# Which PSUM bank a small matrix product gets: in turn, or whichever has been free longest

## The chip, the cores and the metric

The kernel runs on one core of a Trainium2 chip, in float32 (the matmul operands are split into a rounded high part and a low remainder). The metric is the device time of one execution in microseconds (us). Three runs of the kernel before took 1197.13, 1197.44 and 1198.53 us; the median, 1197.44, is the time that the prediction is made for.

## The reference, cut to what matters

Four layers are applied to `x`, 2048 positions by 576 channels: A, B, A, B, each with its own layer norm and a residual.

```python
def A(x):   # Fourier mixing: only the real part is kept
    a, b = x @ dft_hid_re.T, x @ dft_hid_im.T
    return dft_seq_re @ a - dft_seq_im @ b
def B(x):   # gate by a long convolution; k, v, filters do not depend on x
    kv = shift_conv(k, 4 taps) * v
    y = irfft(rfft(kv, 4096) * rfft(ssm_k, 4096))[:2048] + kv * ssm_D
    return x * y
x = x + A(layernorm(x)); x = x + B(layernorm(x))
x = x + A(layernorm(x)); x = x + B(layernorm(x))
```

The convolution result `y` is the same in both B layers, so it is made once.

## The kernel before, in words

TensorE does all transforms as matmuls (line 75, the helper `mm`). PSUM has eight banks of 128 x 512 float32 here: four accumulators `s0` to `s3` and one for the remaining channels, `rm`, serve the large sequence transform (128x512 products, tiles `s` and `rm` in the profile). The last three banks, `bk`, serve every **small product**:

- `f1_products` (line 436): the first transform stage of the convolution. Two banks at once, six matmuls on half the rows of the array, evacuated by ScalarE (line 448). 52 pairs in the first 200 us.
- the middle of the convolution, for 64 blocks of the spectrum: `mid_kernel` (a product `pk`, evacuated by ScalarE through `act`, line 509, then three more ScalarE copies), `mid_signal` (a product `px`, read by three VectorE multiplications with the filter from `mid_kernel`, lines 528 to 530) and, two blocks later, `mid_inverse` (a product `pv`, evacuated by ScalarE, line 509, and stored to DRAM). Three matmuls of 288 columns each.
- `i2_products`: the last stage of the convolution, six matmuls, evacuated by ScalarE (line 509).
- `hidden`: the channel transform of a finished block of rows, 27 matmuls of 288 columns, added to the residual by VectorE (line 284). Two halves per block of 128 rows, in both A layers.
- the remainder accumulators `rem` of the second A layer (`strassen`), which hold a bank for several steps.

Before the change `bank()` (line 79) hands out three tiles, made once for the whole kernel, in turn: the product with number p in the program takes bank p mod 3, whatever the others do. It can start when the product p-3 has been read out.

The order of the work has two parts. The program's text interleaves the streams by hand: the loop over the large transform's steps n (16 per half block) calls the small work from generators (`br` for the convolution, `pending` for `hidden`), with counts such as `MID_FROM = 47` and `I2_FIRST = 37`. From this text the language's planner fixes, ahead of the run, the order of instructions on each engine: by its own reckoning of times it takes, of the instructions whose operands and banks are ready, the one that stands earliest in the text. So a large matmul of a later step goes ahead of a small product that still waits, and products may start in another order than they stand. At run time every engine works its list strictly in that order, with semaphores for what it needs. `behind(...)` adds an order on one engine: all `act` instructions of the middle run on ScalarE in the order of the text.

At the end of a half block (n = 47, 79, 111) the large transform cannot go on until the `hidden` halves of the block before have read the tile `u` that it will overwrite; the loop calls all that are left there.

Of the kernel before, what the change touches and what calls it, by code (L numbers as in the profile page):

```python
# [10 lines left out]
F32 = mybir.dt.float32  # L11
# [4 lines left out]
P = 128  # L16
# [5 lines left out]
NT = 512  # L22
# [43 lines left out]
def fnet_h3_kernel(ctx: ExitStack, tc: tile.TileContext, x, c_mat, w_re, w_im, k_pad, v, shift_k,  # L66
# [4 lines left out]
    psp = ctx.enter_context(tc.tile_pool(name="psp", bufs=1, space=bass.MemoryType.PSUM))  # L71
    dr = ctx.enter_context(tc.tile_pool(name="dr", bufs=1, space=bass.MemoryType.DRAM))

    def mm(ps, lhsT, rhs, first, last, more=False):
        return nc.tensor.matmul(ps, lhsT, rhs, start=first, stop=last, skip_group_check=more).ins  # L75

    banks, given = [psp.tile([P, NT], F32, tag=f"b{i}", name=f"bk{i}") for i in range(3)], [0]

    def bank():
        given[0] += 1  # L80
        return banks[(given[0] - 1) % 3]

    acc4 = [psp.tile([P, NT], F32, tag=f"s{i}", name=f"s{i}") for i in range(4)]
    last_pair = [acc4[2:]]
# [13 lines left out]
    @contextmanager  # L98
    def behind(*instructions):
        with ExitStack() as stack:  # L100
            for i in instructions:
                stack.enter_context(tc.issue_after(i))
            yield
# [36 lines left out]
    def two(v):  # L140
        return v.rearrange("p (a n) -> p a n", a=2)
# [131 lines left out]
    def hidden(us, tb, jj, xres, done, late=False):  # L273
        j = TB * tb + jj
        r = ring["res"]()
        (load_after if late else nc.sync.dma_start)(r, xres(j))
        for hf in range(2):
            ps = bank()
            cs = slice(hf * HD, (hf + 1) * HD)
            for ch in range(9):  # L280
                for n, (a, b) in enumerate(((0, 0), (0, 1), (1, 0))):
                    mm(ps[:, :HD], us[ch][:, a, jj * P:(jj + 1) * P], W[ch][:, b, cs],
                       ch == 0 and n == 0, ch == 8 and n == 2)
            added[:] = [nc.vector.tensor_tensor(r[:, cs], r[:, cs], ps[:, :HD], OP.add).ins]  # L284
            yield
        done(j, r)
# [59 lines left out]
    def branch():  # L346
# [89 lines left out]
            return tuple(paired)  # L436

        def f1_products(j, fc, xf, at, n, so, to):
            ps = [bank()[:, :n] for _ in range(2)]
            last = seq[-1:]  # L440
            for k, (a, b) in enumerate(((0, 1), (0, 0), (1, 0))):
                for i in (1, 0):
                    half = slice(i * HP, (i + 1) * HP)
                    with behind(*last):
                        last = [mm(ps[i], fc[half, a, :], xf[b][half, at:at + n], k == 0, k == 2)]
            so = two(ring[so]())
            for i in range(2):
                stored[:] = [nc.scalar.activation(so[:, i, :], ps[i], AF.Copy).ins]  # L448
            nc.scalar.dma_start(t_d[:, j::J, to:to + n], so)

        conv, made_ops, visits = convolve(), 0, []
        def visit(half):
            if visits and visits[0][0] <= half:
                f1_products(*visits.pop(0)[1:])
# [42 lines left out]
        def mid_half(df, o):  # L497
            ps = bank()
            mm(ps[:, :HD], mc[:, 0, :], df[0][:, o:o + HD], True, False)
            mm(ps[:, :HD], mc[:, 0, :], df[1][:, o:o + HD], False, False)  # L500
            mm(ps[:, :HD], mc[:, 1, :], df[0][:, o:o + HD], False, True)
            return ps
# [653 lines left out]
```

## Time and profile before

| what | before |
|---|---|
| median of three runs | 1197.44 us |
| the profiled execution's own time | 1199.58 us |
| its span, first to last instruction | 1197.8 us |
| TensorE (PE) busy | 1175.3 us, 6248 matmuls |
| VectorE (DVE) / ScalarE (ACT) busy | 839.2 / 660.5 us |
| granted TensorE clock, mean | 0.998 |
| small products `bk`: PE busy | 464.4 us |

The profile is of one execution. Each row of the timeline merges neighbouring instructions of a kind: start, time, engine, line, tiles written <- read, count, and in brackets the engine's idle time before it and what ended it. Matmuls overlap in the array, so a row's time is longer than what it adds; the pace is read from one row's start to the next. PEld is the weight load that goes before each matmul. A wait of PEld that fits under the matmul still running costs nothing.

### The profile page before, as it was taken

To read this page: it belongs to the slowest core of one execution; us is meant where nothing else is said; L and a number is where in the kernel's file an instruction comes from. 1 tells how busy PE (TensorE), PEld (TensorE's weight loads), DVE (VectorE), ACT (ScalarE), POOL (GpSimd) and SP (SyncE) were. 2 spreads that over 40 slices of the span, in tenths; PEclk is the share of its full clock that TensorE was granted. 3 is DMA by queue.
4 is the path that set the end of the run, shared out by engine and by line. 5 is a ranking of instruction groups with operands and counts; after the bars stand their busy time and mean duration, and the time that the engine had idled before them with its cause. 6 is when DMAs were issued, how large, how long until landed. Compare 5 with 4: busy or idle time off the path is not lost.

```text
span 1197.8 us, 18057 instructions
## 1 busy us (share of the span) xinstructions
PE 1175.3 (98%) x6248; PEld 996.6 (83%) x6248; DVE 839.2 (70%) x1498; ACT 660.5 (55%) x1311; POOL 75.1 (6%) x116
## 2 busy tenths in 40 slices
PE   7999999999999999999999999999999999999997
PEld 5776667888888888888988898888888888789997
DVE  7899983679777677675347766865776777774764
ACT  7865555669877668775435666634444445450210
POOL 2210000000000000001101121000000000001111
PEclk9999999999999999999999999999999999999999
DMA  9869898446656667648957676872772787795621
GB/s 337 294 196 315 260 300 268 158 133 182 221 189 199 212 174 209 199 138 270 289 200 237 222 256 216 272 259 71 224 277 71 218 278 257 242 317 173 218 88 41
DMA packets 142845, 259.84 MB, mean 217 GB/s; under 512 B 15649, under 2 KB 43553, under 8 KB 142754
## 3 DMA queue, kind: packets, MB, share of 16 engines
q1 hardware_dynamic: 102674, 205.45, 52.9%
q10 hardware_dynamic: 33168, 42.63, 10.2%
q0 software_dynamic: 6912, 10.62, 3.5%
q8 instruction: 49, 0.80, 0.3%
q14 instruction: 42, 0.34, 0.1%
HBM read 191.99 MB, written 66.65 MB: 216 GB/s over the span
## 4 chain that ended last, share of the span: by engine, by line
PE 76%; ACT 2%; DVE 2%; DMA 1%; issue 1%; POOLq 0%; DVEq 0%; ACTq 0%
PE s L75 42%; PE bk L75 30%; PE rm L75 4%; ACT flts L509 1%; DMA flts<-in_c_mat 0%; ACT u L95 0%; ACT mid L509 0%; DVE u L96 0%; DVE mid L515 0%; DVE flts L529 0%; ACT mats L95 0%; DVE flts L530 0%; DMA xa<-flts 0%; DMA mid<-td 0%; DVE flts L528 0%
## 5 line engine op out<-in xcount | busy, mean ns | idle before, releaser
L75 PE MATMUL s<-mats 128*128 128x512 f32 x2088 | 541.2, 395 | 1.5 <-ACT mats L192 0.9
L75 PEld LDWEIGHTS s<-mats 128*128 128x128 f32 x2088 | 381.4, 188 | 84.1 <-issue 10.9
L96 DVE TENSOR_TENSOR mats<-flts,mats 128x512 fp32r<-128x512 f32 x206 | 140.7, 687 | 64.3 <-ACT mats L95 63.8
L95 ACT ACTIVATE mats<-flts 128x512 fp32r<-128x512 f32 x206 | 128.5, 628 | 85.4 <-PE bk L75 28.4
L75 PE MATMUL bk<-mid 128*128 128x288 f32 x768 | 135.5, 301 | 3.0 <-ACT flts L509 1.6
L75 PEld LDWEIGHTS bk<-mid 128*128 128x128 f32 x768 | 116.9, 188 | 24.1 <-ACT flts L509 7.0
L75 PE MATMUL bk<-w,u 128*128 128x288 f32 x864 | 120.6, 295 | 0.9 <-ACT w L237 0.5
L75 PEld LDWEIGHTS bk<-w,u 128*128 128x128 f32 x864 | 117.8, 188 | 3.5 <-ACT w L237 0.8
L515 DVE TENSOR_TENSOR mid<-flts,mid 128x576 fp32r<-128x576 f32 (+1 forms) x149 | 93.4, 628 | 34.3 <-ACT mid L509 30.5
L509 ACT ACTIVATE flts<-bk 128x288 f32<-128x288 f32 x160 | 62.2, 404 | 88.8 <-PE bk L75 82.4
L75 PE MATMUL rm<-mats 128*128 128x512 f32 x304 | 95.1, 391 | 0.0
L509 ACT ACTIVATE flts<-flts 64x288 f32<-64x288 f32 x192 | 85.0, 443 | 5.5
L509 ACT ACTIVATE mid<-flts 128x576 fp32r<-128x576 f32 (+1 forms) x148 | 80.4, 575 | 7.2 <-DMA flts<-td 3.1
L284 DVE TENSOR_TENSOR flts<-flts,bk 128x288 f32<-128x288 f32 x48 | 21.7, 453 | 69.9 <-PE bk L75 69.9
L448 ACT ACTIVATE flts<-bk 128x384 f32<-128x384 f32 (+1 forms) x104 | 43.1, 462 | 45.7 <-PE bk L75 45.6
L75 PE MATMUL bk<-mats 128*128 128x288 f32 (+1 forms) x376 | 67.8, 317 | 0.0
L75 PEld LDWEIGHTS rm<-mats 128*128 128x128 f32 x304 | 57.1, 188 | 12.1 <-issue 0.2
L75 PE MATMUL s<-t,mats 128*128 128x512 f32 x264 | 65.0, 390 | 0.0
L181 POOL TENSOR_TENSOR flts<-flts 128x1 f32<-128x1 f32 x35 | 28.7, 820 | 523.1 <-DVE flts L180 523.0
L75 PE MATMUL bk<-mats,t 128*128 128x288 f32 (+1 forms) x368 | 59.3, 303 | 0.0
L75 PEld LDWEIGHTS bk<-mats 128*128 128x128 f32 x376 | 55.6, 188 | 3.4
L75 PEld LDWEIGHTS s<-t,mats 128*128 128x128 f32 x264 | 49.4, 188 | 10.6 <-DVE t L96 0.4
(145 smaller groups left out, 1465.3 us busy)
## 6 DMA issues: line engine op xcount, KB each, us to landing
flts<-in_c_mat SPq DMA_DIRECT2D x148, 256.0 KB, 3.5
ph<-in_c_mat SPq DMA_DIRECT2D x54, 512.0 KB, 4.7
flts<-in_c_mat SPq DMA_DIRECT2D x30, 512.0 KB, 5.0
flts<-td SPq DMA_DIRECT2D x53, 288.0 KB, 3.1
td<-flts ACTq DMA_DIRECT2D x36, 384.0 KB, 4.6
vd<-flts ACTq DMA_DIRECT2D x64, 144.0 KB, 2.4
flts<-vd SPq DMA_DIRECT2D x32, 288.0 KB, 4.6
mid<-in_i2c POOLq DMA_DIRECT2D x32, 256.0 KB, 4.9
```

The costliest lines, as they stand in the source:

```text
L75: return nc.tensor.matmul(ps, lhsT, rhs, start=first, stop=last, skip_group_check=more).ins
L95: a = nc.scalar.activation(h, src, AF.Copy).ins
L96: return a, nc.vector.tensor_tensor(l, src, h.bitcast(F32), OP.subtract).ins
L181: pows.append(nc.gpsimd.tensor_tensor(rs, ve, mhalf, OP.pow).ins)
L284: added[:] = [nc.vector.tensor_tensor(r[:, cs], r[:, cs], ps[:, :HD], OP.add).ins]
L448: stored[:] = [nc.scalar.activation(so[:, i, :], ps[i], AF.Copy).ins]
L509: last_act.append(nc.scalar.activation(*args, **kw).ins)
L515: nc.vector.tensor_tensor(l, src, h.bitcast(F32), OP.subtract)
```

## The change

The three fixed tiles stay, renamed `bf`, and `turn()` gives them out to `f1_products` alone. Every other small product asks a pool for a tile with the tag `b`, three at most at a time. The planner then chooses: a product gets a bank when it is its turn to start and a bank of the three has been read out, and the one that has been free longest. No instruction is added or taken away. The eight banks are used up by either scheme, so the pool's tiles can be placed only where the fixed ones have been released, after the first stage's last product.

```diff
-    banks, given = [psp.tile([P, NT], F32, tag=f"b{i}", name=f"bk{i}") for i in range(3)], [0]
-
-    def bank():
+    banks, given = [psp.tile([P, NT], F32, tag=f"b{i}", name=f"bf{i}") for i in range(3)], [0]
+
+    def turn():
         given[0] += 1
         return banks[(given[0] - 1) % 3]
+
+    def bank():
+        return psp.tile([P, NT], F32, tag="b", bufs=3, name="bk")
...
         def f1_products(j, fc, xf, at, n, so, to):
-            ps = [bank()[:, :n] for _ in range(2)]
+            ps = [turn()[:, :n] for _ in range(2)]
```

## The prediction, made before the run

> **What bounds the kernel now.** I read the page first: the span, the busy times and the chain of work that ended last.
>
> ```profile
> span 1197.8 us, 18057 instructions
> PE 1175.3 (98%) x6248; PEld 996.6 (83%) x6248; DVE 839.2 (70%) x1498; ACT 660.5 (55%) x1311; POOL 75.1 (6%) x116
> PE 76%; ACT 2%; DVE 2%; DMA 1%; issue 1%; POOLq 0%; DVEq 0%; ACTq 0%
> ```
>
> TensorE is busy for 98% of the span and the chain runs through it: PE is the bound, and the number of matmuls (6248) does not change. So the change is worth only the time in which PE stands still for a bank. Where that is, the busy time by stage tells (the first three rows: start:end, length, PE, PEld, DVE, ACT, POOL, clock, DMA; the last is the same for instructions on `bk` alone).
>
> ```profile
> 215.00:262.00 47.00, 44.91 (x301) 40.67 (x299) 32.57 (x67) 30.84 (x68) 0.00 (x0) 1.00 0.44 145
> 262.00:330.00 68.00, 67.59 (x351) 57.83 (x351) 57.29 (x114) 59.67 (x130) 0.00 (x0) 1.00 0.61 192
> 612.00:800.00 188.00, 188.00 (x932) 161.05 (x931) 125.74 (x282) 105.71 (x206) 18.80 (x32) 1.00 0.72 239
> ...
> 215.00:262.00 47.00, 40.57 (x274) 36.94 (x272) 15.40 (x35) 6.96 (x17) 1.00 0.44 145
> ```
>
> From 612 to 800 us PE has no gap at all. Between 215 and 262 us 274 of its 301 matmuls write a shared bank, and there it idles most. The first stage keeps its fixed banks, and it ends before the others begin:
>
> ```profile
> L75 PE MATMUL bk<-f1r x312: 286/333/606, 6.6 to 198.1; 64*128 64x384 f32 x108, 64*128 64x288 f32 x48
> L448 ACT ACTIVATE flts<-bk x104: 388/487/501, 9.4 to 198.8; 128x384 f32<-128x384 f32 x72, 128x288 f32<-128x288 f32 x32
> L509 ACT ACTIVATE flts<-bk x160: 387/410/423, 218.2 to 612.3; 128x288 f32<-128x288 f32 x160
> L528 DVE TENSOR_TENSOR flts<-bk,flts x64: 445/456/458, 220.0 to 546.0; 128x288 f32<-128x288 f32 x64
> L529 DVE TENSOR_TENSOR flts<-bk,flts x64: 458/459/462, 220.5 to 546.9; 64x288 f32<-64x288 f32 x64
> L530 DVE TENSOR_TENSOR flts<-bk,flts x64: 450/451/454, 220.9 to 547.4; 64x288 f32<-64x288 f32 x64
> L284 DVE TENSOR_TENSOR flts<-flts,bk x48: 442/453/456, 216.4 to 1161.5; 128x288 f32<-128x288 f32 x48
> ```
>
> The last four kinds are what frees a bank later on: 0.41 us on ScalarE for `pk`, `pv` and the last stage, 0.456 + 0.459 + 0.451 = 1.37 us on VectorE for `px`, 0.45 us for `hidden`. Who waits for them between 199.8 and 620 us, matmuls and weight loads:
>
> ```profile
> PE bk L75 <- ACT flts L509: 1.6, 5, 0.5
> PE bk L75 <- DVE flts L284: 0.8, 1, 0.8
> PE bk L75 <- DVE flts L530: 0.3, 1, 0.3
> ...
> PEld bk L75 <- ACT flts L509: 7.0, 18, 0.8
> PEld bk L75 <- DVE flts L530: 4.4, 14, 0.7
> PEld bk L75 <- DVE flts L284: 1.5, 2, 1.2
> PEld bk L75 <- DVE mid L515: 1.1, 5, 0.2
> ```
>
> 34 weight loads wait for a read-out (18 + 14 + 2, 12.9 us). That is a ceiling: part of it passes under matmuls still running. What is really lost I take from the pace.
>
> ```profile
> 207.07 2.88 PE L75 MATMUL s<-mats 128*128 128x512 f32 x12
> 209.79 0.62 PE L75 MATMUL rm<-mats 128*128 128x512 f32 x2
> ...
> 240.46 3.77 PE L75 MATMUL bk<-w,u 128*128 128x288 f32 x27
> 244.06 0.29 PE L75 MATMUL bk<-mid 128*128 128x288 f32 x1
> ```
>
> A large matmul takes (209.79 - 207.07) / 12 = 0.227 us, a small one (244.06 - 240.46) / 27 = 0.133 us. Now one wait of the kind that the change is about:
>
> ```profile
> 333.40 1.07 PE L75 MATMUL s<-mats 128*128 128x512 f32 x4
> 334.78 0.66 PE L75 MATMUL bk<-mid 128*128 128x288 f32 x3 [0.31 <-DVE flts L530]
> 335.28 1.09 PE L75 MATMUL s<-mats 128*128 128x512 f32 x4
> ...
> 333.11 0.69 ACT L509 ACTIVATE flts<-bk 128x288 f32<-128x288 f32 x2
> ...
> 333.31 0.46 DVE L528 TENSOR_TENSOR flts<-bk,flts 128x288 f32<-128x288 f32 x1
> 334.28 0.45 DVE L530 TENSOR_TENSOR flts<-bk,flts 64x288 f32<-64x288 f32 x1
> ```
>
> The four large matmuls let PE go at 333.40 + 4 x 0.227 = 334.31; the small one starts at 334.78, when line 530 has ended (334.73): **0.47 us lost**. The three then take 0.50 instead of 0.40 us: 0.10 more, since weights are not loaded ahead during a stall. And ScalarE had emptied the two other banks by 333.80, almost 1 us earlier. The product stood before the wrong door.
>
> In the stage of the `hidden` halves it looks otherwise:
>
> ```profile
> 244.19 0.40 PE L75 MATMUL rm<-mats 128*128 128x512 f32 x1
> 244.86 1.06 PE L75 MATMUL bk<-mid 128*128 128x288 f32 x6 [0.27 <-ACT flts L509]
> 246.15 0.53 PE L75 MATMUL bk<-mid 128*128 128x288 f32 x2 [0.24 <-ACT flts L509]
> ...
> 244.40 0.41 ACT L509 ACTIVATE flts<-bk 128x288 f32<-128x288 f32 x1 [1.26 <-PE bk L75]
> ...
> 244.26 0.46 DVE L284 TENSOR_TENSOR flts<-flts,bk 128x288 f32<-128x288 f32 x1 [1.22 <-PE bk L75]
> 245.57 0.45 DVE L530 TENSOR_TENSOR flts<-bk,flts 64x288 f32<-64x288 f32 x1
> ```
>
> PE is free at 244.19 + 0.227 = 244.42 and waits 0.44 us, but the earliest read-out ends at 244.72 (line 284), the next at 244.81 (line 509), the third at 246.02 (line 530): all three banks are held. Choice alone wins 0.1 us here.
>
> Worked so, 17 of the 34 waits delay PE by 0.1 us or more, the first and the last of them these:
>
> ```profile
> 216.92 0.40 PE L75 MATMUL bk<-mid 128*128 128x288 f32 x1 [0.77 <-DVE flts L284]
> ...
> 429.63 0.67 PE L75 MATMUL bk<-mid 128*128 128x288 f32 x3
> ```
>
> Together 5.66 us, and 17 restarts of 0.104 us, 1.77 us: **7.4 us is all that banks cost after the first stage**. By kind: (a) 6 waits with another bank already empty, 1.42 us and 0.62 us of restarts, 2.05 us; (b) 4 waits of the `hidden` stage between 244 and 253 us with all banks held, 1.89 and 0.42, 2.3 us; (c) 7 others with all banks held, 2.34 and 0.73, 3.1 us.
>
> **The change part by part.** *First stage.* Same tiles in the same turn: 0 us. *Handing over.* The pool's first product can start once a fixed bank is released, at about 198.8 + 0.49 = 199.3 us; the first `hidden` product starts at 210.25. 11 us of cover: 0. *Instructions, DMAs, queues.* None is added; SP's and POOL's lists hold the same DMAs, and the stores on ScalarE's queue follow the same read-outs: 0 by themselves. *The turn goes.* The six waits of (a) end: -2.05 us. Those of (c) stay, as no bank is free: 0.
>
> *The planner's order.* This is the part that the trace of before does not show. A product no longer has to follow number p-3, so the planner may start them in another order, and the list of every engine can shift. In (b) a `hidden` half stands earlier in the text than the `pk` and `px` that overtook it because its fixed bank was held; with any bank it goes at the first release, and its 27 matmuls (3.6 us) give ScalarE and VectorE time to empty the others. The bounds: -2.3 us (all of (b)) and, the other way, the price of the slower rival below, +12.3 us. Rows nearest to it are the four waits themselves, so I take half of them, -1.15 us.
>
> *What is late next.* A product that gets its bank earlier may find its operands late. The nearest row is the wait for line 515, the low part of an operand: 5 times, 1.1 us, 0.22 us each. For the ten products of (a) and (b) that is 0 to 2.2 us; as such a wait mostly passes under the matmul before, I take 0.5 us.
>
> *Behind a waiting product* stands everything on PE, in its fixed order; nothing on the other engines is queued behind it except the read-outs of that product.
>
> One rule of the Trainium skill speaks against (a). The page Perfetto Trace Analysis, section Optimization Strategy, says that a gap which keeps recurring can mean that there is not enough PSUM for the next tile, and points to the number of buffers. The number stays three here, so by that rule the gain would be 0 and the time 1197.4 us. For (b) and (c) the trace agrees: all three were held. For (a) it does not: two of three were empty at 333.80.
>
> **The sum** against the profiled execution: 1199.58 - 2.05 - 1.15 + 0.5 = 1196.9 us. That execution stands 2.14 us above the median of the runs, 1197.44; for a run I therefore forecast **1194.7 us**, 0.23% less.
>
> **The rivals.**
> *All bank waits go* (the new order also clears (b) and (c)): 1197.44 - 7.4 = 1190.0 us. For it: from 215 to 262 us the `hidden` halves are ready filling work. Against it: in 11 of 17 waits no bank was empty, and three banks remain three.
>
> *Nothing changes*: the read-outs finish mostly in turn, so the bank free longest is the one whose turn it is; or the six waits become waits for operands. 1197.4 us. For it: 11 of the 17 waits, and 17 of 34 that cost nothing today. Against it: the six rows like 334.78. The Trainium skill's page Perfetto Trace Analysis, section Matmuls, asks that independent groups rotate through the banks, which the fixed turn already does; by that alone there is nothing to win.
>
> *Slower: `px` takes the banks ahead of `pv`.* With fixed banks, between 262 and 550 us, `px`, `pk` and `pv` each keep to one bank. From a pool the `pk` and `px` of the next block take banks as soon as their operands are split, and a `pv` that becomes ready next finds none until a `px` has gone through lines 528 to 530: 1.37 us. ScalarE must read that `pv` before the next `pk`, so the chain of the middle is stretched too. It counts only where PE has no large matmul to fill with, above all from 215 to 262 us: 274 matmuls there, less 7 halves of 27 and a few that are left of the first, are about 81, or 27 products of three, 9 blocks. 9 x 1.37 = 12.3 us if each is exposed; with half of that 1197.4 + 6 = 1203.4 us, at most 1209.7. It decides from the point where a `pv` wait outlasts the matmuls that are ready behind it in the list. For it: VectorE and ScalarE work 57 and 60 of 68 us from 262 to 330, so read-outs do queue. Against it: `pv` stands earlier in the text, so it wins whenever it is ready at the release.
>
> **How the numbers follow.** A measurement of this kernel can tell about 0.2%, 2.4 us, from no change. Forecast case 0.45 (1192.5 to 1196.8; 0.27 of it faster by over 0.2%, 0.18 within); all waits gone 0.10, faster; nothing changes 0.12 (0.02, 0.08, 0.02); slower 0.33 (0.02 within, 0.31 slower). Faster 0.39, same 0.28, slower 0.33. The range goes from just under the best case, 1189.5, to 1205.5, past the middle of the slower case; what it leaves out is the tail up to 1209.7.
>
> **What would show it.** Right: PE's waits for line 530 in 330 to 440 us gone, the gaps between 244 and 253 us shorter, the first stage unchanged up to 198 us, and PE still without a gap from 612 to 800 us. Wrong: new gaps of PE with `pv` products behind line 530, PE's waits for line 515 growing past 2 us, large matmuls (`s`, `rm`) waiting for line 95 or 515 because the lists of ScalarE and VectorE shifted, or gaps after 612 us, where I assume none.

## The result and the profile after

Over nine runs of each on the same chip the changed kernel took 1195.03 us (1193.42 to 1195.99) and the kernel before 1198.53 us (1197.13 to 1199.86). The ratio is 0.9970, with a 95% interval from 0.9960 to 0.9981: 3.6 us less, at least 2.3 and at most 4.8. A second comparison, seven runs against 25, gave 0.9968 (0.9957 to 0.9979). Forecast were 1194.7 us and a gain of 2.7 us.

The page of the changed kernel: its profiled execution took 1195.03 us.

```profile
span 1193.3 us, 18055 instructions
PE 1172.4 (98%) x6248; PEld 996.3 (83%) x6248; DVE 840.3 (70%) x1498; ACT 661.1 (55%) x1311; POOL 75.6 (6%) x116
PE 76%; ACT 3%; DVE 1%; issue 1%; DMA 0%; POOLq 0%; ACTq 0%; DVEq 0%; SPq 0%
```

PE is still busy for 98% and still carries 76% of the chain. A change of 0.3% can't be seen on the page; the table by stage shows it (same columns as before the change):

```profile
215.00:262.00 47.00, 46.01 (x309) 42.42 (x308) 35.84 (x73) 32.51 (x71) 0.00 (x0) 1.00 0.48 153
262.00:330.00 68.00, 67.61 (x350) 57.58 (x349) 56.49 (x111) 59.48 (x128) 0.00 (x0) 1.00 0.58 183
612.00:800.00 188.00, 188.00 (x928) 160.85 (x927) 128.10 (x285) 107.49 (x209) 18.80 (x32) 1.00 0.73 244
800.00:1050.00 250.00, 250.00 (x1103) 206.54 (x1102) 176.56 (x234) 113.64 (x187) 0.00 (x0) 1.00 0.63 209
```

In the stage of the `hidden` halves PE now does 309 matmuls where it did 301, with 46.01 us busy instead of 44.91. From 262 to 330 us (67.61 us busy, 67.59 before) and from 612 to 800 us (188.00 in both) PE's busy time has not moved. One row is a surprise. From 800 to 1050 us PE has no idle time left, and in the kernel before it had 1.09 us there:

```profile
800.00:1050.00 250.00, 248.91 (x1098) 205.70 (x1097) 174.52 (x232) 113.74 (x188) 0.00 (x0) 1.00 0.63 206
```

Who the weight loads wait for between 199.8 and 620 us (us in total, times, longest):

```profile
PEld bk L75 <- ACT flts L512: 7.6, 19, 0.8
...
PEld bk L75 <- DVE mid L518: 1.0, 4, 0.3
...
PEld bk L75 <- DVE flts L533: 0.5, 2, 0.3
```

All lines of the changed kernel stand three further down, so L533 is the old line 530 and L512 the old 509. The waits behind line 530 fell from 14 (4.4 us) to two (0.5 us). Those behind the read-outs of ScalarE did not fall: 18 with 7.0 us became 19 with 7.6 us. Both rows are the case in small: a product no longer stands before the slowest door, but it often stands before another.

**Where the time went** is counted best at points where both kernels have issued exactly the same set of matmuls: the start of the next one, changed kernel less kernel before. I did this for three pairs of profiles, the first and two repetitions of both kernels.

| stretch (time in the kernel before) | first pair | second | third |
|---|---|---|---|
| 217 to 258 us (260 in the first pair): `hidden` stage | -2.00 us | -2.00 | -1.96 |
| 258 to 590 us | -0.53 | -0.08 | -0.61 |
| 590 to 1040 us | +0.23 | +0.87 | +0.57 |
| 1040 to 1050 us | -1.28 | -1.26 | -1.02 |

Before that the pairs differ by -0.7 to +2.7 us, both ways, through loads at the start and a wait for the splitting of weights at 213 us (lines 237 and 238), which is longer in one execution than in the next. In the second pair the changed kernel lost 0.4 us between 462 and 471 us, which hides its gain in the second row. What the third row loses is lost at one place: at 749 us in the second and third pair (0.86 and 0.57 us), at 863 us in the first (0.2 us). The lists of all engines are the same there in both kernels, and no run shows why.

### The profile page after: what moved, and what is told of

Same layout as the page of the kernel before. It is cut to its first block, busy times and chain, and to the rows that moved or that the text cites. A ratio compares the mean times of both kernels' runs of the same rounds, so it can differ in the third digit from the quotient of the medians.

```text
span 1193.3 us, 18055 instructions
## 1 busy us (share of the span) xinstructions
PE 1172.4 (98%) x6248; PEld 996.3 (83%) x6248; DVE 840.3 (70%) x1498; ACT 661.1 (55%) x1311; POOL 75.6 (6%) x116
## 4 chain that ended last, share of the span: by engine, by line
PE 76%; ACT 3%; DVE 1%; issue 1%; DMA 0%; POOLq 0%; ACTq 0%; DVEq 0%; SPq 0%
PE s L75 43%; PE bk L75 30%; PE rm L75 4%; ACT flts L512 1%; ACT mid L512 1%; ACT u L98 0%; DMA wd<-w 0%; ACT mats L98 0%; DVE mid L518 0%; DVE flts L534 0%; DVE flts L533 0%; DVE flts L531 0%; DVE flts L532 0%; DVE mats L99 0%; POOLq L1155 0%
## 5 line engine op out<-in xcount | busy, mean ns | idle before, releaser
L75 PE MATMUL bk<-mid 128*128 128x288 f32 x768 | 131.9, 298 | 2.4 <-ACT flts L512 1.6
L512 ACT ACTIVATE flts<-bk 128x288 f32<-128x288 f32 x160 | 62.1, 404 | 86.8 <-PE bk L75 77.7
L512 ACT ACTIVATE flts<-flts 64x288 f32<-64x288 f32 x192 | 85.0, 443 | 5.5
L512 ACT ACTIVATE mid<-flts 128x576 fp32r<-128x576 f32 (+1 forms) x148 | 80.4, 575 | 7.6 <-DMA flts<-td 3.2
L451 ACT ACTIVATE flts<-bf 128x384 f32<-128x384 f32 (+1 forms) x104 | 43.2, 463 | 45.6 <-PE bf L75 45.5
```

Of the source, the lines that this page charges most:

```text
L512: last_act.append(nc.scalar.activation(*args, **kw).ins)
```

## The experiments

Twelve experiments ran, four of them repeats of the two kernels, in four groups, each group on one chip with its own runs of the kernel before (medians 1198.36 to 1198.95 us; the group of the last profile has a single one).

**Both kernels once more.** No edit.

> The kernel before, profiled once more. In its first profile TensorE lost 0.68 + 0.66 us at 213.7 and 214.5 us to the weight splits (lines 237 and 238) and 1.25 us at 1045.8 us to line 96 of the second A layer; in the changed kernel's profile these are 0.18 + 0.66 us and 0. Theory 'chance of one execution': the wait at 1045 us is under 0.3 us or at another place this time, and the first one moves by some tenths. Rival 'the banks of the remainder accumulators cause it': it stands again at the same place with 1.0 to 1.5 us. The 17 bank waits (5.7 us together) repeat within 0.3 us under both.

> The changed kernel once more, for its time beside the next two on the same chip: 3 to 4 us under the kernel before (ratio 0.9965 to 0.9975) under every theory. Its profile should again show no wait of 1 us near 1041 us if the rival 'banks of the remainder accumulators' holds; under 'chance of one execution' a wait of that kind may come up at any step of the second A layer.

The kernel before: span 1195.9 us, with the wait at 1045 us again. The changed kernel: ratio 0.9968 (0.9957 to 0.9979), without it. The `hidden` stage was 2.00 us shorter. So the gain and its place repeat.

**The pool from 262 us on.** The first 36 small products after the first stage (they reach to the end of the `hidden` stage) keep the turn:

```diff
     def bank():
-        return psp.tile([P, NT], F32, tag="b", bufs=3, name="bk")
+        small[0] += 1
+        return turn() if small[0] <= 36 else psp.tile([P, NT], F32, tag="b", bufs=3, name="bk")
```

> One part of the change alone: the fixed turn also serves the first 36 small products after the first stage (the stage of the first eight hidden halves, up to about 262 us); the pool serves the rest. Theory H (the gain is made where the hidden halves stand without large matmuls to fill in): 0.3 to 0.9 us faster than before, the waits between 244 and 253 us stand as before. Rival A (the prediction's term a, products before the wrong door after 262 us): 1.5 to 2.1 us faster. If the wait at 1045 us comes from the banks of the remainder accumulators, another 1.2 us faster under both.

**The pool up to 262 us.** The first 36 come from the pool, the rest take a second fixed set in turn:

```diff
     def bank():
-        return psp.tile([P, NT], F32, tag="b", bufs=3, name="bk")
+        small[0] += 1
+        if small[0] <= 36:
+            return psp.tile([P, NT], F32, tag="b", bufs=3, name="bk")
+        if not second:
+            second.extend(psp.tile([P, NT], F32, tag=f"c{i}", name=f"bg{i}") for i in range(3))
+        return second[small[0] % 3]
```

> The other part alone: the pool serves the first 36 small products after the first stage, three fixed banks in turn the rest, the remainder accumulators of the second A layer too. Theory H: 2.0 to 2.8 us faster than before, with the waits between 244 and 253 us gone and those from 330 to 430 us standing as before. Rival A: 0.5 to 1.2 us faster. Together with late_pool it should make up the whole change's 3 to 4 us; what is missing in the sum belongs to chance or to a coupling of the two stages.

The pool late took 1197.73 us, ratio 0.9991 (0.9982 to 1.0000); the pool early 1196.96 us, ratio 0.9989 (0.9977 to 1.0001). These times don't separate the parts, the profiles do. The stage from 215 to 262 us in the repeated kernel before, with the pool late, and with the pool early:

```profile
215.00:262.00 47.00, 45.50 (x302) 41.53 (x303) 33.27 (x69) 31.89 (x71) 0.00 (x0) 1.00 0.46 147
```

```profile
215.00:262.00 47.00, 45.42 (x303) 41.15 (x301) 33.22 (x68) 30.90 (x68) 0.00 (x0) 1.00 0.46 146
```

```profile
215.00:262.00 47.00, 46.73 (x314) 43.09 (x313) 35.80 (x74) 32.50 (x71) 0.00 (x0) 1.00 0.49 153
```

The early pool issues 314 matmuls in the stretch, the late one 303, like the kernel before. Counted at equal work against the repeated kernel before, the early pool goes from +0.41 us at 215 us to -1.59 us at 258, a gain of 2.0 us, gives back 0.3 us up to 275 us (-1.34), and stays within 0.1 us of that up to 1040 us. The late pool loses nothing between 258 and 275 us, so this loss comes with the new order of the `hidden` stage. The late pool then goes from +1.03 at 275 us to +0.35 at 590, a gain of 0.7 us. Up to 1050 us the two win another 0.9 us (early) and 1.3 us (late) at 1045 us, where their instructions are those of the kernel before. So nearly three quarters of what the order of the banks brings arise in 45 us of the run. In time the late pool agrees with its 0.7 + 1.3 us (1.1 us measured, at most 2.2); the early pool's 2.0 - 0.3 + 0.9 us lie at the edge of its interval (1.3 us measured, at most 2.8).

**The pool in the first stage too.**

```diff
         def f1_products(j, fc, xf, at, n, so, to):
-            ps = [turn()[:, :n] for _ in range(2)]
+            ps = [bank()[:, :n] for _ in range(2)]
```

> The pool for the first stage too: f1_products asks bank() for its two tiles, no fixed tile is left. Theory 'the bank that has been free longest helps wherever products queue': the first stage has 4 waits of 0.1 us or more for its read-out (2.3 us in the changed kernel), so up to 2 us faster than the change, 5 us under before. Rival 'in the first stage the turn is already the order in which banks come free' (both products of a pair are read by one engine, in order): within 1 us of the change, first stage unchanged to 198 us.

1201.12 us, ratio 1.0019 (1.0010 to 1.0028), some 6 us above the changed kernel: neither expectation held. At equal work with the changed kernel 2.9 us were lost between 147 and 163 us alone (the 3.6 us in the next expectation also hold a difference that stood before 147 us); another 2.1 us were lost between 314 and 530 us, whose cause no run shows. To see whether the first loss is the pool's own price there, the reverse of the change was run, **the pool in the first stage alone**, the turn from then on:

```diff
-    def bank():
-        return psp.tile([P, NT], F32, tag="b", bufs=3, name="bk")
+    bank = turn
...
-            ps = [turn()[:, :n] for _ in range(2)]
+            ps = [psp.tile([P, NT], F32, tag="b", bufs=3, name="bk")[:, :n] for _ in range(2)]
```

> The pool serves the first stage alone, and from then on the fixed banks in turn: the reverse of the change. Theory P (from a pool the two products of a pair, on opposite halves of the rows of the array, no longer start side by side, which is what cost some 3.6 us between 150 and 166 us in the kernel with the pool everywhere): 2.5 to 4.5 us more than the kernel before, all of it between 145 and 170 us, and after 200 us a constant difference to the kernel before; about 1201 to 1203 us where that one stands at 1198.7. Theory Q (the loss there belongs to the order of the lists that the pool everywhere gave, and not to the pairs): within 1 us of the kernel before.

1202.22 us, ratio 1.0035 (1.0023 to 1.0047), 4.2 us slower, as theory P expected; against the first profile of the kernel before it goes from -0.02 us at 147 us to +0.68 at 152 and +2.88 at 163, 2.9 us that the profile shows, and from 275 to 1040 us the difference is constant within 0.05 us. The cause stands in the timeline of PE, here with the pool in the first stage:

```profile
158.47 0.79 PE L75 MATMUL bk<-f1r 64*128 64x384 f32 x5
159.19 0.96 PE L75 MATMUL s<-mats 128*128 128x512 f32 x3
...
160.54 0.43 PE L75 MATMUL bk<-f1r 64*128 64x384 f32 x1
160.90 1.21 PE L75 MATMUL s<-mats 128*128 128x512 f32 x4
```

and here the same six matmuls in the kernel before:

```profile
159.83 0.79 PE L75 MATMUL bk<-f1r 64*128 64x384 f32 x6
160.55 1.89 PE L75 MATMUL s<-mats 128*128 128x512 f32 x7
```

The two products of a pair use the upper and the lower 64 rows of the array (`64*128`) and write two banks. With fixed banks their six matmuls alternate and take 160.55 - 159.83 = 0.72 us. From the pool five go and the sixth comes alone: 0.72 + (160.90 - 160.54) = 1.08 us, 0.36 us more for such a pair. Five such lone matmuls stand between 146 and 164 us and none in the kernel before; the 2.9 us are 0.6 us for each, the 0.36 us and some 0.2 us beside it. The Trainium skill (TensorE: Matmul & The Clock Gate, section The mechanism) says that matmuls on different row groups run at the same time but never out of program order; the trace agrees with the first, since six cost no more than five of which one has no partner, and no row here tests the second. The turn in the first stage is therefore not an idle remnant: it keeps the partners together.

**Two banks in the pool**, to price a bank:

```diff
-        return psp.tile([P, NT], F32, tag="b", bufs=3, name="bk")
+        return psp.tile([P, NT], F32, tag="b", bufs=2, name="bk")
```

> The change with a pool of two banks after the first stage in place of three. It puts the price on a missing bank and forces the slower rival: px and pk of one block hold both, pv finds none. Theory 'banks, not operands, are what small products wait for in the hidden stage': 8 to 30 us slower than the change, nearly all lost between 200 and 560 us, nothing from 612 us on. Rival 'operands': under 3 us slower.

1203.72 us, ratio 1.0036 (1.0023 to 1.0049): some 8 us above the changed kernel, lost between 213 and 560 us, none from 612 us on. The waits of the weight loads, 199.8 to 620 us:

```profile
PEld bk L75 <- DVE flts L533: 10.7, 22, 0.9
PEld bk L75 <- ACT flts L512: 4.1, 10, 0.7
```

With a bank less, `px` with its three readers on VectorE is what the products wait for most: 22 times, and twice with three banks. This is the queue that the slower rival of the prediction feared.

**A bank of its own for `hidden`**, first with a pool of two for the others, then with two fixed ones in turn:

```diff
     def bank():
-        return psp.tile([P, NT], F32, tag="b", bufs=3, name="bk")
+        return psp.tile([P, NT], F32, tag="b", bufs=2, name="bk")
...
-            ps = bank()
+            ps = psp.tile([P, NT], F32, tag="h", bufs=1, name="bk")
```

```diff
     def bank():
-        return psp.tile([P, NT], F32, tag="b", bufs=3, name="bk")
+        other[0] += 1
+        return banks[1 + other[0] % 2]
...
-            ps = bank()
+            ps = banks[0]
```

> hidden gets a bank of its own, the other small products a pool of two. Theory D (the hidden stage gains because a hidden half no longer waits behind a px for its own door): the stage from 215 to 262 us is as fast as in the change or within 1 us, since the half finds its bank empty after line 284 (0.45 us); but after 262 us the middle has two banks and loses 2 to 8 us by 560 us. Rival N (the stage gains because three doors are open to everyone): the stage itself is as slow as before or slower.

> hidden gets a fixed bank of its own, the other small products two fixed banks in turn. Theory D: from 215 to 262 us as fast as in the change or within 1 us, without any pool; after 262 us slower than hidden_own_pool, as px, pk and pv now alternate between two doors of which a px holds one for 2 to 3 us: 5 to 15 us lost by 560 us. Rival N: slower than before in the first of these stretches too.

They took 1231.69 us (ratio 1.0269, 1.0250 to 1.0287) and 1250.11 us (1.0428, 1.0407 to 1.0448). About 30 us of that is a thing that both expectations overlooked: in the last stage 32 `hidden` halves follow each other, and with one bank each waits for the read-out of the one before. In the first of the two, from 1050 us on:

```profile
PE bk L75 <- DVE flts L287: 12.4, 16, 3.5
PE bk L75 <- DVE ph L287: 9.4, 15, 1.8
```

What they were made for is seen before 560 us. With the pool of two, the `hidden` stage is as quick as with the changed kernel (309 matmuls in both), though `hidden` may touch only one bank:

```profile
215.00:262.00 47.00, 46.47 (x309) 43.21 (x310) 36.13 (x74) 32.30 (x71) 0.00 (x0) 1.00 0.49 153
```

So it isn't the access to three banks that counts there. A bank of its own for the half is not enough either: with the other two in turn the stage issues 302 matmuls, about as in the kernel before, and loses 1.6 us to the changed kernel by 259 us, against theory D:

```profile
215.00:262.00 47.00, 45.91 (x302) 41.81 (x303) 33.52 (x70) 32.55 (x71) 0.00 (x0) 1.00 0.48 148
```

What the two quick kernels share, as far as these runs show, is that no product of the stage takes turns with one of another kind. From 217 to 560 us the kernel with the pool of two lost 4.7 us to the changed one, as theory D expected; the one with two in turn lost 19.2 us, more than expected, and another 4.9 us between 612 and 1040. There the weight loads wait 81 times for ScalarE's read-outs (`act` is line 515 in that kernel) between 199.8 and 620 us, and only 11 times for the last reader of `px` (line 536):

```profile
PEld bf L75 <- ACT flts L515: 31.1, 81, 0.9
PEld bf L75 <- DVE flts L536: 4.2, 11, 0.6
```

With two banks for the other products, taking whichever is free is worth 14 us up to 560 us; with three for all, 2.5 us.

**A fourth bank**, the one of `rm`, put into the pool:

```diff
     def bank():
-        return psp.tile([P, NT], F32, tag="b", bufs=3, name="bk")
+        return psp.tile([P, NT], F32, tag="b", bufs=4, name="bk")
...
-                ps.append(psp.tile([P, NT], F32, tag="rm", name="rm"))
+                ps.append(psp.tile([P, NT], F32, tag="b", bufs=4, name="rm"))
```

> The bank that the fifth product of a large step (rm) has for itself is put into the same pool, so that the small products can take a fourth bank while no rm is live, and an rm product takes one of the four. Theory F (what is left of the waits after 262 us is a shortage: all three banks held): the waits at 356, 370, 384 and 426 us (0.36 us each and 0.10 of restart), those at 270 and 413 and the ones of the hidden stage at 252 to 258 us get shorter or go: 1 to 3 us less than the changed kernel, at about 1192 to 1194 us where that one stands at 1195. Theory G (the order of the waiting products is what holds them, a fourth bank is filled with the next pk or px at once and an rm that needs a bank finds none): no gain, or 1 to 4 us more, with matmuls of rm waiting for a read-out of bk.

1194.96 us, ratio 0.9970 (0.9959 to 0.9980), the same as the changed kernel. Of the waits that theory F wanted shorter, the one at 270 us is gone (0.4 us at equal work), which the time doesn't show; the others are there as they were. Here is one (compare the rows of the changed kernel at 355.96 below):

```profile
353.33 1.99 PE L75 MATMUL s<-mats 128*128 128x512 f32 x8
355.54 0.67 PE L75 MATMUL bk<-mid 128*128 128x288 f32 x3 [0.22 <-ACT flts L512]
```

But neither theory was really tested: an `rm` accumulates through nearly all of this stretch (140 of its matmuls between 199.7 and 619.7 us), so the fourth bank is mostly taken and the small products have three as before. That more banks would end the remaining waits stays open; no bank is left to try it with.

**Both kernels a third time**, for the wait at 1045 us.

> The kernel before once more, for the wait of PE at about 1045 us (1.25 and 1.1 us in its two profiles, none in the profiles of the kernels with a pool). Theory S (it belongs to the kernel before: its large load lands later there): again 1.0 to 1.3 us at 1045 us. Theory T (it comes and goes between executions): less than 0.5 us here.

> The changed kernel a third time, for the wait of PE at about 1045 us, which stands in all three profiles of the kernel before (1.25, 1.1 and 0.8 us) and in neither of the changed kernel's two. Theory S (it belongs to the kernel before): again none here. Theory T (it comes and goes with the landing of one load of in_c_mat, by the execution): between 0 and 1.2 us, above 0.3 us one time in three. By both theories the stretch from 216 to 258 us is 2.0 us shorter than in the profiles of the kernel before.

Two rows of the first profile of the kernel before, and two of its third:

```profile
1044.34 0.39 PE L75 MATMUL s<-mats,t 128*128 128x512 f32 x1
1045.82 1.43 PE L75 MATMUL s<-mats,t 128*128 128x512 f32 x5 [1.09 <-DVE mats L96]
```

```profile
1042.70 0.39 PE L75 MATMUL s<-mats,t 128*128 128x512 f32 x1
1043.72 3.51 PE L75 MATMUL s<-mats,t 128*128 128x512 f32 x14 [0.63 <-DVE mats L96]
```

After one matmul (0.227 us) PE waits 1045.82 - 1044.57 = 1.25 us, and 0.79 us in the third profile. The changed kernel, first and third profile, runs through:

```profile
1041.30 4.34 PE L75 MATMUL s<-mats,t 128*128 128x512 f32 x18
```

```profile
1040.18 4.24 PE L75 MATMUL s<-mats,t 128*128 128x512 f32 x18
```

That makes three of three against none of three, with 0.3 us in the kernel with the pool in the first stage alone and in the one with two banks. The instructions of all engines are the same there in both kernels. What differs first is how long a load of `in_c_mat` that SyncE issues at the same place, some 22 us before the wait, takes to land: 5.2, 5.1 and 4.1 us in the kernel before, 3.7, 3.5 and 3.7 us in the changed one. That the wait follows from it is not shown. Theory T's one in three is not excluded by three profiles, theory S fits better, and neither says why the load is slower. **The cause stays open**; it is worth 1.0 to 1.3 us of the 3.6.

## Why the prediction came out right, and where its working did not

**The number was right, two of its terms were not, and that it fits so closely is luck.** 1195.03 us stands 0.3 us from the forecast. But the forecast counts from 1197.44 us, the median of three runs, and nine runs of the same kernel gave 1198.53: the gain was 3.6 us and not 2.7. It is also made up otherwise. The forecast had 2.05 us for (a), 1.15 for (b) and 0.5 against them. The profiles show about 0.8, 2.0 and nothing, with 0.3 us given back after the `hidden` stage, 0.2 to 0.9 lost between 590 and 1040 us, and 1.0 to 1.3 won at a place that the forecast held for finished.

**(a) Six waits before the wrong door: forecast -2.05 us, measured -0.8.** The six stand between 330 and 431 us, and over this stretch the three pairs agree: -0.82, -0.80 and -0.83 us. The table's second row is smaller because it holds the 0.3 us lost up to 275 us. The model wait at 334.78 us went as described. In the changed kernel:

```profile
331.01 0.84 PE L75 MATMUL s<-mats 128*128 128x512 f32 x3
331.69 0.55 PE L75 MATMUL bk<-mid 128*128 128x288 f32 x3
332.08 1.54 PE L75 MATMUL s<-mats 128*128 128x512 f32 x6
```

331.01 + 3 x 0.227 = 331.69: no wait, and the three take 0.39 us. At equal work this place gave -0.55 us (from -2.42 to -2.97), the 0.47 + 0.10 us of the prediction. The others did not follow. Here is one of them, in the kernel before:

```profile
356.78 2.21 PE L75 MATMUL s<-mats 128*128 128x512 f32 x9
358.98 1.37 PE L75 MATMUL bk<-mid 128*128 128x288 f32 x6
360.19 0.85 PE L75 MATMUL s<-mats 128*128 128x512 f32 x3
```

and in the changed kernel, PE and then the read-outs of two of the three banks:

```profile
353.76 2.00 PE L75 MATMUL s<-mats 128*128 128x512 f32 x8
355.96 0.66 PE L75 MATMUL bk<-mid 128*128 128x288 f32 x3 [0.20 <-ACT flts L512]
356.45 0.40 PE L75 MATMUL s<-mats 128*128 128x512 f32 x1
...
355.52 0.69 ACT L512 ACTIVATE flts<-bk 128x288 f32<-128x288 f32 x2
...
356.03 0.45 DVE L533 TENSOR_TENSOR flts<-bk,flts 64x288 f32<-64x288 f32 x1
```

Before: 356.78 + 9 x 0.227 = 358.82, so the first product is 0.16 us late, and the six matmuls take 1.21 instead of 0.80 us; 0.57 us in all. After: 353.76 + 8 x 0.227 = 355.58, the product is 0.38 us late, and its three take 0.49 instead of 0.40; 0.47 us. The planner, free to choose, moved the product one large matmul forward, to where all three banks were held: the first read-out on ScalarE ends near 355.92, the second later, line 533 at 356.48. Two short waits became one longer one, and the gain is 0.1 us. The same holds at 370 and 384 us; at 426 us nothing was gained, and at 413 us the wait grew from 0.22 to 0.34 us. The step that failed is "the six waits of (a) end". I took the order of the matmuls as given for (a) while I let the planner change it for (b). The page of the Trainium skill that I set against (a) (Perfetto Trace Analysis, section Optimization Strategy: a recurring gap can mean too little PSUM) was nearer to the truth for these five than I was, though no run had a free fourth bank there to test it. At 334.78 us and in the `hidden` stage it was not: time was won with the same three banks.

**(b) The waits of the `hidden` stage: forecast half of 2.3 us, measured 1.96 to 2.00.** The mechanism was the one named, a half that starts at the first release and covers the read-outs; only the size was off. One block in the kernel before, then one in the changed kernel with its read-outs:

```profile
246.52 3.71 PE L75 MATMUL bk<-w,u 128*128 128x288 f32 x27
250.07 0.30 PE L75 MATMUL bk<-mid 128*128 128x288 f32 x1
250.87 1.05 PE L75 MATMUL bk<-mid 128*128 128x288 f32 x6 [0.50 <-ACT flts L509]
252.16 0.53 PE L75 MATMUL bk<-mid 128*128 128x288 f32 x2 [0.24 <-ACT flts L509]
252.52 3.76 PE L75 MATMUL bk<-w,u 128*128 128x288 f32 x27
```

```profile
242.85 3.83 PE L75 MATMUL bk<-w,u 128*128 128x288 f32 x27
246.51 1.38 PE L75 MATMUL bk<-mid 128*128 128x288 f32 x9
247.73 0.40 PE L75 MATMUL s<-mats 128*128 128x512 f32 x1
247.97 3.87 PE L75 MATMUL bk<-w,u 128*128 128x288 f32 x27
...
242.38 0.41 ACT L512 ACTIVATE flts<-bk 128x288 f32<-128x288 f32 x1 [1.42 <-PE bk L75]
...
242.93 0.45 DVE L533 TENSOR_TENSOR flts<-bk,flts 64x288 f32<-64x288 f32 x1
```

A block has 27 + 9 small matmuls, 36 x 0.1335 = 4.81 us. Before, it lasts 252.52 - 246.52 = 6.00 us: 1.2 us of waiting. After, it lasts 247.97 - 242.85 = 5.12 us with one large matmul (0.227) more: 0.1 us of waiting. The half at 242.85 starts 0.06 us after ScalarE has emptied a bank (242.38 + 0.41 = 242.79), while line 533 still reads `px` until 243.38. Then its 3.6 us of matmuls cover all read-outs, and the next three products run without a gap. Half of the bound was a choice for want of a row; the rows that were quoted beside it (3.6 us of cover for 1.37 us of read-out) spoke for nearly the whole.

**The rest of the sum.** The first stage, forecast at 0: -0.18 us by 157 us in the first pair, no effect. Handing over, forecast at 0: nothing beside the weight splits at 213 us, which vary by themselves. Late operands, forecast at +0.5 us: PE's delay behind line 518 is one of 0.16 us at 254.76, so about 0. The seven waits of (c), forecast to stay: their kind is what remains; the one at 273.14 us, 0.56 us late, stands in the changed kernel three large matmuls earlier, 0.55 us late at 269.98 us. The 1045 us place is named nowhere in the prediction: "gaps after 612 us" were to show it wrong. A gap of the kernel before went there, and small ones of the changed kernel at 749 or 863 us came, which by its own words speak against it.

**The rivals.** That all bank waits go fell with the 7.6 us behind line 512. That nothing changes fell by the interval, though for five of the six waits of (a) it was nearly so. The slower one, `px` ahead of `pv`, did not happen: only two waits, 0.5 us together, stand behind line 533. But its fear was not empty: with a pool of two banks 22 waits, 10.7 us, stand there and the kernel is some 8 us slower. The third bank is what kept the queue behind `px` away.

## What to carry to other kernels

Count a wait "before the wrong door" as won only if the planner can't move the waiting instruction; where it can, ask what will be held at the place to which it moves. Buffers from a pool paid here where products of unequal read-out share few of them; the fixed turn paid where products must start side by side, as pairs on opposite halves of the array. The gaps next to a long independent piece of work were worth nearly their whole length (2.0 of 2.3 us) as soon as that piece could go first.

## What was not expected of the hardware

- Six 64-row matmuls of 384 columns in pairs take 0.72 us, and 1.08 us when the last pair is parted.
- A stalled product pays a restart: three small matmuls take 0.49 or 0.50 us after a wait and 0.39 or 0.40 us without one.
- A load of 512 KB, issued at the same place of the same lists, landed after 3.5 to 5.2 us; in the three profiles where it took 4.1 us or more, PE later stood still for 0.8 to 1.25 us.
